# A fused attention and gated MLP block: the second x tile is issued from GpSimd's DMA queue instead of SyncE's

## The chip, the core and the metric

The kernel runs on one core of a Trainium2 chip. A core has five engines with a queue of instructions each: TensorE (PE; its weight loads are listed as PEld), VectorE (DVE), ScalarE (ACT), GpSimd (POOL) and SyncE (SP), which only issues DMAs. SyncE, ScalarE and GpSimd can all issue DMAs; sixteen DMA engines carry them out. In the profile q1 is the queue of SyncE's DMAs, q10 that of ScalarE's and q0 that of GpSimd's. The metric is the device time of one execution in microseconds, as the median of several runs; lower is better. The profile is of one execution.

## What is computed

x has 2048 rows of 640 (bfloat16). The block adds to x a sliding dilated attention and a gated MLP, both on the normalised x:

```python
xn = _layernorm(x)                 # mean and variance over the 640 columns, no weights
qkv = xn @ wqkv                    # 640 x 1920; 32 heads of 20
idx = pos[:, None] - arange(8) * 2 # each row attends to itself and 7 earlier ones, 2 apart
attn = softmax(q . k[idx] * 20 ** -0.5)
A = (attn . v[idx]) @ wo           # 640 x 640
B = ((xn @ w_gate) * (xn @ w_up)) @ w_down   # 640 x 1536, 640 x 1536, 1536 x 640
return x + A + B
```

## The kernel before

Rows are worked on in 16 tiles of 128 (TS), columns of x in 5 chunks of 128 (NCH). The time falls into stages on TensorE, in this order: a start with dummy matmuls and the first tiles; the projections to Q, K and V; gate and up of the MLP, during which VectorE does the attention; the down projections with the output projection of the attention; the stores. No loop is left on the chip. Every operation is recorded in program order by `op` (line 97), which derives its waits from the tiles that it reads and writes; `emit` (line 158) then writes each engine's own list in that order. So an engine's instructions run in the order in which the program records them for that engine, and every DMA has a semaphore of its own that its readers wait on.

The start of the program, to which the change belongs:

- VectorE clears ZERO, EPSC, IDENT, KH's and VO's padding, MASK and MSK0 (lines 297 to 306). GpSimd turns IDENT into an identity matrix and MSK0 into a mask with one affine_select each (lines 300 and 307). Before these it has only four small constant memsets, and after them nothing until it issues the accumulating DMAs of the attention (`acc`, line 532).
- XST holds the x tiles in 13 slots. x tile 0 is loaded in two halves, one from SyncE and one from ScalarE (lines 325 to 327). Then SyncE issues, one after the other: x tile 1 (line 328, by `x_load` of line 310), the five chunks of the Q weights (`wqkv_load(0, c)`), x tiles 2 and 3, the five chunks of the K weights, x tiles 4 to 7, the V weights in one DMA, and x tiles 8 to 12. None of these waits for anything. Each goes through the helper `dma` (line 293), so that the profile lists all of them under L294. Each x tile and each weight chunk has 160 KB. Behind them on SyncE stand the DMA transposes of tile 4 and later (L423).
- TensorE begins with nine dummy matmuls on ZERO (`warm(9)`, L453). The layer norm of tile 0 runs on VectorE (statistics L372 and L378, L384, reciprocal L404, scaling L419), with the square root on ScalarE (L385). TensorE then transposes the five chunks of tile 0 with the help of IDENT (`ln_pe`, L434), and VectorE copies them into XNT (L445).
- The statistics of tile 1 are ScalarE's work: `ln_sums` takes the sum (L392), the sum of squares (L394) and the square root (L397) from XST's slot 1; VectorE follows with the reciprocal and the scaling in two parts (L419, 256 and 384 columns).
- `proj_tile(0, 0, ...)` (L492) multiplies tile 0 with the Q weights: chunk after chunk, five matmuls each, 25 in all. Just before the five of the last chunk the program places `tr(1)`, the transposes of tile 1 and their copies. Then `proj_tile(0, 1, ...)` does the same for tile 1, and the loop at L773 multiplies tiles 0 and 1 with the K weights, with the transposes of tiles 2 and 3 in between.

Of the kernel before, what the change touches and what calls it, by code (L numbers as in the profile page):

```python
# [21 lines left out]
TS = 128  # L22
# [19 lines left out]
class Sched:  # L42
# [54 lines left out]
    def op(self, eng, fn, r=(), w=(), dma=False, name="", group=None, event=None):  # L97
        X = _Op()
        X.eng, X.fn, X.name, X.dma = eng, fn, name, dma
        X.needs_tick, X.event, X.pre_know, X.idx = False, None, None, len(self.ops)  # L100
        rk = [k for a in r for k in self.keys(a)]
        wk = [k for a in w for k in self.keys(a)]
        deps = {}
        inorder = eng in ("pe", "act", "dve")
        for k in rk:
            st = self.state.get(k)
            if st is not None:
                for o in st[0]:
                    deps[o.idx] = o
        for k in wk:  # L110
            st = self.state.get(k)
            if st is None:
                continue
            if group is not None and st[2] == group and not st[1]:
                for o in st[3]:
                    deps[o.idx] = o
                continue
            for o in st[0]:
                if not (eng == "pe" and o.eng == "pe"):
                    deps[o.idx] = o  # L120
            for q in st[1]:
                if eng in ("pe", "act") and q.eng == eng and not q.dma:
                    continue
                deps[q.idx] = q
        last = {}
        keep = []
        for d in deps.values():
            if d.dma or d.eng == "pool":
                keep.append(d)
            else:  # L130
                b = last.get(d.eng)
                if b is None or b.idx < d.idx:
                    last[d.eng] = d
        X.deps = keep + list(last.values())
        for d in X.deps:
            if not d.dma:
                d.needs_tick = True
        for k in rk:
            st = self.state.get(k)
            if st is None:  # L140
                self.state[k] = [[], [X], None, []]
            elif inorder and st[1] and st[1][-1].eng == eng and not st[1][-1].dma:
                st[1][-1] = X
            else:
                st[1].append(X)
        for k in wk:
            st = self.state.get(k)
            if group is not None and st is not None and st[2] == group and not st[1]:
                st[0].append(X)
            else:  # L150
                before = [] if st is None else st[0] + st[1]
                self.state[k] = [[X], [], group, before]
        if dma:
            X.event = event or self.dma_event(1)
        self.ops.append(X)
        return X
# [55 lines left out]
def build_kernel(nc, A_x, A_wqkv, A_wo, B_x, B_w_gate, B_w_up, B_w_down, out):  # L212
    K = Sched(nc)
    op = K.op
# [3 lines left out]
    def sb(name, shape, dtype=BF16, at=None):  # L218
        n = mybir.dt.size(dtype)
        for s in shape[1:]:  # L220
            n *= s
        n = (n + 63) // 64 * 64
        if at is None:
            at = place[0]
            place[0] += n
        assert at + n <= 229344, (name, at + n)
        return K.sbuf(name, shape, dtype, at)
# [37 lines left out]
    XST = sb("XST", [128, NXS, D], at=a_log)  # L265
# [24 lines left out]
    xhbm = A_x[0]  # L290
    ohbm = out[0]

    def dma(o, i, r=(), w=(), name="", eng="sp", group=None):
        return op(eng, lambda e: e.dma_start(o, i), r=r, w=w, dma=True, name=name, group=group)  # L294


    op("dve", lambda e: e.memset(ZERO[:], 0.0), w=[ZERO[:]], name="zero")  # L297
    op("dve", lambda e: e.memset(EPSC[:], EPS), w=[EPSC[:]], name="epsc")  # L298
    op("dve", lambda e: e.memset(IDENT[:], 0.0), w=[IDENT[:]], name="ident0")
# [10 lines left out]
    def x_load(t, eng="sp"):  # L310
        dma(XST[:, t % NXS, :], xhbm[t * TS:(t + 1) * TS, :], w=[XST[:, t % NXS, :]], name=f"xld{t}", eng=eng)
# [13 lines left out]
    for half, eng in ((0, "sp"), (1, "act")):  # L325
        dst = XST[:, 0, half * DHALF:(half + 1) * DHALF]
        dma(dst, xhbm[0:TS, half * DHALF:(half + 1) * DHALF], w=[dst], name=f"xh{half}", eng=eng)
    x_load(1)
    for c in range(NCH):
        wqkv_load(0, c)  # L330
    x_load(2)
# [622 lines left out]
def bass_parallel_sum__sliding_local_dilated__glu_gated_bilinear__prompt_kernel(  # L954
    nc, A_x, A_wqkv, A_wo, B_x, B_w_gate, B_w_up, B_w_down, out
):
    build_kernel(nc, A_x, A_wqkv, A_wo, B_x, B_w_gate, B_w_up, B_w_down, out)
# [28 lines left out]
```

## Time and profile before

| what | value |
|---|---|
| median of 4 runs | 252.63 us (252.48 to 252.7) |
| the profiled execution | 252.6 us |
| its span, first to last instruction | 251.3 us |
| mean granted TensorE clock | 1.000 |
| TensorE's idle time listed by its own waits | 1.0 us, at the start |
| weight loads' idle time listed before 8 us | 1.0 + 2.0 (dummy matmuls), 0.9, 0.2 us |
| GpSimd busy before 40 us | four memsets and two affine_selects (0.29 and 0.33 us) |
| DMA from SyncE's queue in the first 30 us | 10400 packets, 6.47 MB |

The table's busy shares and waits are of one execution. The page cuts the span in 40 slices of 6.28 us; the first one, to which the change belongs, and the two after it look like this (start of each row of the page, busy share in tenths):

| row | slices 1 to 3 |
|---|---|
| PE | 8 9 9 |
| DVE | 5 8 9 |
| ACT | 5 4 8 |
| POOL | 1 0 0 |
| DMA | 6 9 9 |

A line of the timeline gives the start and the duration in us, the engine, the line of the program, the operation, what it writes and reads, and how many instructions are merged; in brackets stand the idle time of that engine before it and what ended it. Issues of DMAs are marked by SPq, ACTq or POOLq; their duration is that of the issue and not of the transfer. The time from issue to landing comes from the DMA view.

### The profile page before, as it was taken

How to read it: one execution, taken by the hardware profiler on the slowest of the kernel's cores; microseconds unless marked ns; L12 is line 12 of the kernel's file. 1: busy time of each engine (PE TensorE's matmuls, PEld its weight loads, DVE VectorE, ACT ScalarE, POOL GpSimd, SP SyncE). 2: the span in 40 equal slices, each digit the busy share in tenths (PEclk: the TensorE clock that was granted, in tenths of full speed). 3: DMA queues.
4: the chain of work that ended last, by engine and by line, in shares of the span. 5: the costliest groups of instructions: out<-in, count | busy, mean ns of one | idle time of the engine just before them, and what ended most of it. 6: DMA issues, size and time to landing. Idle time of an engine off the chain costs nothing.

```text
span 251.3 us, 3265 instructions
## 1 busy us (share of the span) xinstructions
PE 248.4 (99%) x1294; PEld 129.2 (51%) x1294; DVE 215.9 (86%) x255; ACT 114.6 (46%) x203; POOL 32.6 (13%) x41
## 2 busy tenths in 40 slices
PE   8999999999999999999999999999999999999997
PEld 3995555555544444444444444444444444445775
DVE  5899889999999963999999994899999999996212
ACT  5487657555555557555555552325555111011000
POOL 1000001044434231002231101002000000200200
PEclk9999999999999999999999999999999999999999
DMA  6999879764787462355369972197500011490551
GB/s 179 318 279 198 102 194 408 180 115 87 134 147 129 83 122 45 125 211 102 66 125 261 383 231 42 37 332 62 93 0 3 21 29 34 57 134 21 81 153 52
DMA packets 33776, 33.78 MB, mean 134 GB/s; under 512 B 17985, under 2 KB 30273, under 8 KB 33729
## 3 DMA queue, kind: packets, MB, share of 16 engines
q1 hardware_dynamic: 27280, 24.13, 34.3%
q0 software_dynamic: 6192, 9.31, 22.9%
q8 instruction: 10, 0.16, 0.3%
q10 hardware_dynamic: 288, 0.13, 0.2%
q14 instruction: 6, 0.04, 0.0%
HBM read 14.42 MB, written 4.59 MB: 76 GB/s over the span
## 4 chain that ended last, share of the span: by engine, by line
PE 99%; DVE 0%; issue 0%
PE PS L638 41%; PE PS L665 22%; PE PS L475 21%; PE PS L697 7%; PE PS L499 2%; PE PS L453 2%; PE PS L492 1%; PE PS L773 1%; PE PS L434 1%; DVE FOUT L701 0%; DVE ZERO L297 0%; DVE EPSC L298 0%
## 5 line engine op out<-in xcount | busy, mean ns | idle before, releaser
L638 PE MATMUL PS<-XNT,WG 128*128 128x512 bf16 x240 | 59.6, 379 | 0.0
L638 PE MATMUL PS<-XNT,WU 128*128 128x512 bf16 x240 | 59.6, 379 | 0.0
L475 PE MATMUL PS<-XNT,WQKV 128*128 128x512 bf16 x250 | 54.1, 379 | 0.0
L605 DVE TENSOR_TENSOR PVB<-VO,ATB 128x10240 f16<-128x10240 bf16 x8 | 43.9, 5489 | 0.2
L475 PEld LDWEIGHTS PS<-XNT,WQKV 128*128 128x128 bf16 x250 | 29.4, 118 | 24.4
L640 ACT ACTIVATE USX<-PS 128x512 bf16<-128x512 f32 x48 | 28.7, 597 | 22.6 <-PE PS L638 22.6
L638 PEld LDWEIGHTS PS<-XNT,WU 128*128 128x128 bf16 x240 | 23.5, 98 | 28.3
L638 PEld LDWEIGHTS PS<-XNT,WG 128*128 128x128 bf16 x240 | 23.5, 98 | 28.3
L600 DVE TENSOR_TENSOR PVB<-PVB 128x5120 f16<-128x5120 f16 (+1 forms) x16 | 34.5, 2156 | 0.3
L533 POOL DMA_DIRECT2D LOG<-PE x24 | 21.9, 925 | 58.4 <-DMA LOG<-PE 58.4
L640 ACT ACTIVATE HT<-PS 128x512 bf16<-128x512 f32 x36 | 21.5, 597 | 16.4 <-PE PS L638 16.4
L671 ACT ACTIVATE DT<-PS 128x512 f16<-128x512 f32 x15 | 8.9, 596 | 42.5 <-PE PS L665 42.5
L665 PE MATMUL PS<-HT,WD 128*128 128x512 bf16 x120 | 27.5, 379 | 0.0
L522 DVE TENSOR_TENSOR TMP<-QH,KH 128x2048 f16<-128x2048 bf16 x16 | 19.2, 1219 | 1.0 <-ACT KH L482 0.9
L665 PEld LDWEIGHTS PS<-HT,WD 128*128 128x128 bf16 x120 | 11.7, 98 | 14.2
L522 DVE TENSOR_TENSOR PP<-QH,KH 128x2048 f16<-128x2048 bf16 x16 | 18.9, 1219 | 0.0
L665 PE MATMUL PS<-VO,WO 128*128 128x512 bf16 x75 | 18.6, 379 | 0.0
L527 DVE TENSOR_TENSOR PP<-PP,TMP 128x4096 f16<-128x4096 f16 x8 | 18.3, 2291 | 0.2
L701 DVE TENSOR_TENSOR FOUT<-PS,XR 128x320 bf16<-128x320 f32 (+2 forms) x9 | 4.1, 455 | 15.3 <-PE PS L697 15.3
L533 POOL DMA_DIRECT2D PE<-PP x8 | 8.3, 1043 | 63.3 <-DVE PP L528 63.3
L482 ACT ACTIVATE VO<-PS 128x512 bf16<-128x512 f32 x20 | 11.9, 597 | 8.5 <-PE PS L475 8.5
L643 DVE TENSOR_TENSOR HT<-HT,USX 128x512 bf16<-128x512 bf16 x36 | 14.3, 417 | 1.7 <-ACT USX L640 1.7
(71 smaller groups left out, 222.1 us busy)
## 6 DMA issues: line engine op xcount, KB each, us to landing
PE<-PP POOLq DMA_DIRECT2D x8, 512.0 KB, 4.8
ATB<-LOG SPq DMA_DIRECT2D x8, 512.0 KB, 4.9
LOG<-PE POOLq DMA_DIRECT2D x24, 128.0 KB, 2.7
WG<-in_B_w_gate_dram SPq DMA_DIRECT2D x1, 1920.0 KB, 8.1
WU<-in_B_w_up_dram SPq DMA_DIRECT2D x1, 1920.0 KB, 14.7
WD<-in_B_w_down_dram SPq DMA_DIRECT2D x1, 1920.0 KB, 11.4
out_dram<-in_A_x_dram SPq DMA_DIRECT2D x1, 1920.0 KB, 10.6
out_dram<-FACC POOLq DMA_DIRECT2D x3, 640.0 KB, 6.9
```

Of the source, the lines that this page charges most:

```text
L475: op("pe", (lambda l, x, c: lambda e: e.matmul(PS[:, b, :], l, x, start=(c == 0), stop=(c == NCH - 1)))(l, x, c), r=[l, x], w=[PS[:, b, :] ...
L482: op("act", lambda e: e.activation(o, PS[:, b, :], ACT.Copy, scale=sc), r=[PS[:, b, :]], w=[o], name=f"pev{which}_{m}_{j}")
L522: return (1.22, lambda: op("dve", lambda e: e.tensor_tensor(o, qw, kw, ALU.mult), r=[q, k], w=[o], name=f"prod{h}_{p}_{c}"))
L527: (2.3, lambda: op("dve", lambda e: e.tensor_tensor(a, a, b, ALU.add), r=[a, b], w=[a], name=f"psum{h}_{p}")),
L533: op("pool", lambda e: e.dma_start(o, i, accum_op=ALU.add), r=[o, i], w=[o], dma=True, name=name)
L600: return lambda: op("dve", lambda e: e.tensor_tensor(o, x, y, ALU.add), r=[x, y], w=[o], name=f"{name}_{b}")
L605: lambda: op("dve", lambda e: e.tensor_tensor(PVB[:], vw, aw, ALU.mult), r=[v, a], w=[PVB[:]], name=f"pv_{b}")),
L638: op("pe", (lambda l, x, c: lambda e: e.matmul(PS[:, b, :], l, x, start=(c == 0), stop=(c == NCH - 1)))(l, x, c), r=[l, x], w=[PS[:, b, :] ...
L640: op("act", lambda e: e.activation(o, PS[:, b, :], ACT.Copy), r=[PS[:, b, :]], w=[o], name=f"guev{which}_{m}_{j}")
L643: h_pending.append(lambda: op("dve", lambda e: e.tensor_tensor(h, h, o, ALU.mult), r=[h, o], w=[h], name=f"h{m}_{j}"))
L665: op("pe", (lambda l, x, i: lambda e: e.matmul(PS[:, b, :], l, x, start=(i == 0), stop=(i == n - 1)))(l, x, i), r=[l, x], w=[PS[:, b, :]], ...
L697: op("pe", (lambda l, x, i, b, wid: lambda e: e.matmul(PS[:, b, 0:wid], l, x, start=(i == 0), stop=(i == n - 1)))(l, x, i, b, wid), r=[l, ...
```

## The change

The load of x tile 1 is taken out of SyncE's list and recorded ahead of everything else as a DMA of GpSimd. It moves the same 128 rows of x to the same slot of XST under the same name, and its readers wait for its semaphore as before. SyncE goes from its half of tile 0 straight to the weights; GpSimd's two affine_selects stand behind the new DMA. Nothing else is changed.

```diff
+    op("pool", lambda e: e.dma_start(XST[:, 1, :], xhbm[TS:2 * TS, :]), w=[XST[:, 1, :]], dma=True, name="xld1")
     op("dve", lambda e: e.memset(ZERO[:], 0.0), w=[ZERO[:]], name="zero")
     op("dve", lambda e: e.memset(EPSC[:], EPS), w=[EPSC[:]], name="epsc")
     op("dve", lambda e: e.memset(IDENT[:], 0.0), w=[IDENT[:]], name="ident0")
...
     for half, eng in ((0, "sp"), (1, "act")):
         dst = XST[:, 0, half * DHALF:(half + 1) * DHALF]
         dma(dst, xhbm[0:TS, half * DHALF:(half + 1) * DHALF], w=[dst], name=f"xh{half}", eng=eng)
-    x_load(1)
     for c in range(NCH):
         wqkv_load(0, c)
```

## The prediction

> **What bounds the kernel now.** I read the page first. TensorE is busy 99% of the span, and the chain that ended last is TensorE from end to end.
>
> ```profile
> PE 248.4 (99%) x1294; PEld 129.2 (51%) x1294; DVE 215.9 (86%) x255; ACT 114.6 (46%) x203; POOL 32.6 (13%) x41
> PE 99%; DVE 0%; issue 0%
> ```
>
> So only something that moves TensorE's own stream can move the end. Next I read the waits of TensorE and of its weight loads: all of them lie in the first 8 us. From 8 us on the matmuls follow each other without a gap (the chain gives 250 of L475 in 53.96 us, 0.216 us each, and the same pace for L638 and L665). What the first 8 us gain or lose is therefore what the end gains or loses, unless later slack swallows it. Third, the timeline of those 8 us (start, duration, engine, idle before and its releaser):
>
> ```profile
> 0.74 0.86 SPq L294 DMA_DIRECT2D XST<-in_A_x_dram  x2
> ...
> 1.65 2.33 SPq L294 DMA_DIRECT2D WQKV<-in_A_wqkv_dram  x5
> ...
> 2.72 0.49 DVE L372 BATCH_NORM_STATS2 STATS<-XST 128x6 f32<-128x320 bf16 x1 [1.42 <-DMA XST<-in_A_x_dram]
> ...
> 3.92 0.29 ACT L385 ACTIVATE SD<-MV,EPSC 128x1 f32<-128x1 f32 x1 [1.68 <-DVE MV L384]
> ...
> 4.12 0.72 ACT L392 ACTIVATE XNS<-XST 128x640 bf16<-128x640 bf16 x1
> ...
> 5.64 1.18 PEld L492 LDWEIGHTS PS<-XNT,WQKV 128*128 128x128 bf16 x15
> ...
> 6.44 0.63 DVE L419 TENSOR_SCALAR XNS<-XST,MV,SD 128x256 bf16<-128x256 bf16 x2
> ...
> 7.03 0.32 PEld L492 LDWEIGHTS PS<-XNT,WQKV 128*128 128x128 bf16 x5 [0.21 <-DVE XNS L419]
> 7.29 0.32 PEld L434 LDWEIGHTS PS<-IDENT,XNS 128*128 128x128 bf16 x5
> ```
>
> SyncE issues half of x tile 0 (0.74), x tile 1 (about 1.2), then the five chunks of the Q weights, 0.47 us apart from 1.65. ScalarE takes the sums of x tile 1 from 4.12; VectorE normalises that tile at 6.44 to 7.07; TensorE transposes it at 7.29. The 0.21 us of idle before 7.03 is put down to VectorE, but those five matmuls (tile 0, chunk 3) don't read what L419 wrote. They read weight chunk 3. Fourth, the DMA view with one issue in each window (operands, queue, count, KB, us from issue to landing): x tile 1, then weight chunks 0, 3 and 4.
>
> ```profile
> XST<-in_A_x_dram SPq DMA_DIRECT2D x1, 160.0 KB, 2.7
> ...
> WQKV<-in_A_wqkv_dram SPq DMA_DIRECT2D x1, 160.0 KB, 2.9
> ...
> WQKV<-in_A_wqkv_dram SPq DMA_DIRECT2D x1, 160.0 KB, 3.9
> ...
> WQKV<-in_A_wqkv_dram SPq DMA_DIRECT2D x1, 160.0 KB, 3.9
> ```
>
> Chunk 3 is issued at about 3.07 and lands at 6.97: that releases 7.03. Chunk 4 (3.54) lands at 7.44, used at 7.57. Tile 1 lands at about 3.9, 0.2 before ScalarE wants it.
>
> **What the Trainium skill says.** "DMA: Bandwidth & Descriptors", Specifications, gives a first byte after about 1 us for a DMA issued by GpSimd and 0.6 us for one of SyncE. The trace has both later: SyncE's issue at 0.74 has its first packets at 1.76; GpSimd's at 51.04, on idle DMA engines, at about 2.45 minus 1.04, that is 1.4 us after its issue. The same page, Queues, rings and completion order, says that a DMA engine goes round the queues packet by packet. The trace agrees only in part: once running, GpSimd's queue shares the engines (56% to 57% from 136.3 to 139.2), but with a deep SyncE backlog it first waits:
>
> ```profile
> DMA packets 986, 1.21 MB, mean 242 GB/s; under 512 B 16, under 2 KB 986, under 8 KB 986
> ...
> q1 hardware_dynamic: 986, 1.21, 88.1%
> ...
> WD<-in_B_w_down_dram SPq DMA_DIRECT2D x1, 1920.0 KB, 11.4
> LOG<-PE POOLq DMA_DIRECT2D x2, 128.0 KB, 7.2
> ```
>
> This is the DMA view from 131.2 to 136.2. A GpSimd DMA was issued at 131.20; in 5 us not one packet of its queue ran. It landed after 7.2 us, where the same 128 KB land after 2.7 us on idle engines:
>
> ```profile
> LOG<-PE POOLq DMA_DIRECT2D x1, 128.0 KB, 2.7
> ```
>
> "SBUF — State Buffer", SBUF: two separate sides, says that VectorE in its two-port modes keeps GpSimd from writing descriptors. VectorE runs only memsets up to 1.3 us and then waits until 2.72; no run here shows such a lock, and I cost it at nothing.
>
> **The change part by part.**
> Removed from SyncE: one issue of 0.47 us. Everything that SyncE issues behind it before its first real wait (five Q chunks, x tiles 2 and 3, five K chunks, the later x tiles, the V weights) is issued 0.47 us earlier; the transposes at 14.04 wait for VectorE and stay with it. Issue isn't landing: the DMA engines are 0.8 to 1.0 busy from 2 us on, and the landings of the five Q chunks (4.55, 5.2, 6.2, 6.97, 7.44) lie up to 1.0 us apart where the issues are 0.47. The bytes in front of chunk 3 are the same before and after. I take 0.1 to 0.3 us of earlier landing for chunks 3 and 4, with 0 and 0.47 as the ends.
>
> What this is worth: if chunk 3 is there at 6.75, its matmuls follow at once (their pitch is 0.055 us), and the transposes of tile 1 could start at 7.03 instead of 7.29: 0.26 us. The next limits are close: the second part of L419 ends at 7.07, wanted by the third transpose at about 7.15, and chunk 4 (7.44, wanted at 7.31). So the gain is 0 to 0.26; I take 0.15. Further on, tile 2 lands at 7.82 and VectorE starts on it at 7.88; tile 2's normalisation ends at 10.31 for a transpose at 10.53; so 0.15 us passes through even if tile 2 lands no earlier. Where it is earlier, VectorE follows. Nothing later takes the gain: the gapless stream starts there.
>
> Added to GpSimd: one DMA issue. GpSimd is free at about 0.7. Issues of 128 KB are 0.86 to 0.88 us; the first one in the trace, of another shape, took 1.02 where its later ones start at 0.84, so I allow 1.05. Behind it in order stand two affine_selects: IDENT's goes from 1.27 to about 1.8, done near 2.1, and its first reader is the transpose at 4.81, 2.7 us of cover; MSK's output is read after 32 us.
>
> Moved: tile 1's data. First packet at 0.7 + 1.4 + 0.2 = 2.3, against about 2.4 before. In front then stand only the two halves of tile 0 (ScalarE's first packets at 2.08, both landed by 3.1) and weight chunk 0, posted at about 1.2 + 1.0 = 2.2. From below: tile 1 goes first and lands as it does now, 3.9. From above within this mechanism: it waits for chunk 0 and then shares with chunk 1. 160 KB at half of about 250 GB/s take 1.3 us, from 3.2, plus 0.3 until the last of 16 engines reports: 4.8. Alternating with chunk 0 from 2.4, by the same rate: 2.4 + 1.3 + 0.3 = 4.0 to 4.4. I take 4.2.
>
> What waits for it: ScalarE's L392 stands first in its queue, so sums, square, square root, then VectorE's reciprocal and L419, then everything of VectorE behind that, go with it. ScalarE is ready at 4.12. Each us past 4.12 moves L419 by as much; against today's 7.40 for the third transpose, L419's 7.13 leaves 0.27 us. So a landing up to 4.39 costs nothing against before, and after that the loss is landing minus 4.39. At 4.2 the loss is nothing; but L419 (7.13 + 0.08) allows a gain of 0.19.
>
> Sum for the profiled execution: 252.6 (span 251.3, and 1.3 around it) minus 0.15 is 252.45. The median of the runs is 252.63, 0.03 above it: 252.5.
>
> **The rivals.**
> A, the forecast: tile 1 lands by 4.4 and the weight wait shrinks, 252.35 to 252.65. For it: little is posted ahead at 2.3.
> B: both queues alternate to tile 1's cost, landing 4.4 to 4.9, lost 0 to 0.5: 252.6 to 253.1. For it: the even sharing seen at 136 us; five chunks follow without a pause. Against it: the shared stretch need only last 160 KB.
> C, the other side: GpSimd's queue is kept out by the SyncE stream. It decides from a landing of 4.9 on (4.39 + 0.5). Place: ScalarE's L392, price 1 us for each us. At 5.5 the end is 252.63 + 1.1 = 253.7; with the whole 7.2 us of issue to landing, 7.9 - 4.39 = 3.5, so 256.1. For it: three GpSimd issues under load (131.20, 132.57, 139.98) landed after 7 to 10 us. Against it: in those, 1.9 MB stood ahead; here some 0.3 MB at most.
> D: it does more than I see, for instance that TensorE's clock comes up earlier against the work. The pitch of the 128-wide matmuls is 0.107 us up to 6.2 and 0.055 after; the skill's "TensorE: Matmul & The Clock Gate", Part 1, calls the moment variable from run to run. The eleven or so matmuls at the slow pitch between 5.1 and 6.25, each 0.05 us dearer, bound this at 0.6 us: 252.0.
> That tile 1 isn't loaded in time for the sum to be right isn't a rival: ScalarE waits for its semaphore.
>
> **How the numbers follow.** A 0.42, B 0.20, C 0.30, D 0.08. About 0.2% (0.5 us) is what a measurement of this kernel can tell from no change. A and B stay within it except for their edges; C is slower; D is faster where it is whole. Faster 0.07, same 0.62, slower 0.31. The range goes from 252.3 (A's best) to 253.5, which takes in B and the near half of C and leaves out about 2 in 10 (most of D, the far end of C). The likeliest case alone has 252.35 to 252.65.
>
> **What would show it.** Tile 1's landing, and the idle before L392: none beyond the wait for the deviation of tile 0 if A holds, 1 us for each us in C. The five weight loads at 7.03 without their 0.21 us. IDENT's affine_select near 1.8 with no one waiting. SyncE's first weight issue at about 1.17. The start of L773 (9.38) earlier by 0.1 to 0.2 in A and later in B and C. The forecast is wrong if tile 1 lands after 4.9, or if chunks 3 and 4 land no earlier and tile 1 later.

## The result, and the profile after

The changed kernel takes 253.12 us (median of 32 runs, 252.57 to 253.72) where the kernel before, in runs beside it, takes 252.54 us (52 runs). The ratio is 1.0022 with a 95% interval of 1.0017 to 1.0027: about 0.6 us slower. The forecast was 252.5 us, a little faster or no change. The measured time lies within the range of 252.3 to 253.5, but on the other side of the kernel before, and clear of it.

The profiled execution took 253.23 us, with a span of 251.9. First the page of the changed kernel, the share of the last chain by engine:

```profile
PE 96%; DMA 2%; ACT 1%; DVE 1%; issue 0%
```

TensorE had 99% of this chain before. Now a DMA is in it. Its chain of waits in order of time (start, length, what) says which:

```profile
1.30 3.84 DMA XST<-in_A_x_dram
5.17 0.84 ACT XNS L392 x2
...
6.03 0.93 ACT XNS L394 x2
...
7.31 0.17 DVE SD L404
...
7.51 0.36 DVE XNS L419
...
7.91 0.28 PE PS L434 x2
```

Until 7.91 the end hangs on the load of tile 1, ScalarE's sums and VectorE's scaling; from there on it is TensorE as before. The timeline of the same kernel answers to the lines shown of the kernel before:

```profile
1.20 2.66 SPq L294 DMA_DIRECT2D WQKV<-in_A_wqkv_dram  x5
...
1.30 0.73 POOL L297 DMA_DIRECT2D XST<-in_A_x_dram  x1 [0.86 <-DVE MSK L307]
...
5.17 0.74 ACT L392 ACTIVATE XNS<-XST 128x640 bf16<-128x640 bf16 x1 [0.87 <-DMA XST<-in_A_x_dram]
...
6.91 0.32 PEld L492 LDWEIGHTS PS<-XNT,WQKV 128*128 128x128 bf16 x5 [0.18 <-issue]
...
7.51 0.64 DVE L419 TENSOR_SCALAR XNS<-XST,MV,SD 128x256 bf16<-128x256 bf16 x2
7.90 0.11 PEld L434 LDWEIGHTS PS<-IDENT,XNS 128*128 128x128 bf16 x2 [0.67 <-DVE XNS L419]
...
10.00 1.16 PEld L773 LDWEIGHTS PS<-XNT,WQKV 128*128 128x128 bf16 x11
```

SyncE's first weight issue starts at 1.20 instead of 1.65, and the weight loads of the chunk 3 matmuls at 6.91 instead of 7.03: this part of the change works. But ScalarE idles for 0.87 us until tile 1 is there and starts its sums at 5.17 instead of 4.12. The transposes of tile 1 follow at 7.90 instead of 7.29. The first K matmul, which closes the disturbed part, has its weight load at 10.00. In the kernel before the same line is

```profile
9.38 1.16 PEld L773 LDWEIGHTS PS<-XNT,WQKV 128*128 128x128 bf16 x11
```

The difference, 0.62 us, is the whole difference of the two profiled executions (253.23 against 252.6), but for 0.01 us. The rest is rigid: from this weight load to the end of the span it is 241.93 us in both.

The DMA view of the changed kernel, at GpSimd's issue, gives the tile's landing (1.30 + 3.8 = 5.1):

```profile
XST<-in_A_x_dram POOLq DMA_DIRECT2D x1, 160.0 KB, 3.8
```

The tile's packets run from 2.94 on. In the DMA view from 2.93 to 4.8, SyncE's queue (q1) has the larger share of the DMA engines beside them (queue, packets, MB, share):

```profile
q1 hardware_dynamic: 312, 0.35, 52.1%
q0 software_dynamic: 48, 0.16, 37.0%
```

### The profile page after: what moved, and what is told of

It reads as the page before. It is cut to its first block, busy times and chain, and to the rows that moved or that the text cites. A ratio compares the mean times of both kernels' runs of the same rounds, so it can differ in the third digit from the quotient of the medians.

```text
span 251.9 us, 3265 instructions
## 1 busy us (share of the span) xinstructions
PE 248.5 (99%) x1294; PEld 129.1 (51%) x1294; DVE 216.0 (86%) x255; ACT 114.6 (45%) x203; POOL 33.0 (13%) x42
## 4 chain that ended last, share of the span: by engine, by line
PE 96%; DMA 2%; ACT 1%; DVE 1%; issue 0%
PE PS L638 41%; PE PS L665 22%; PE PS L475 21%; PE PS L697 7%; PE PS L499 2%; DMA XST<-in_A_x_dram 2%; PE PS L773 1%; PE PS L492 1%; PE PS L434 0%; ACT XNS L394 0%; ACT XNS L392 0%; DVE XNS L419 0%; ACT SD L397 0%; DVE FOUT L701 0%; DVE SD L404 0%
```

## The experiments

In seven more kernels tile 1, or another transfer of the start, goes by another way, and two kernels are profiled a second time. The times are ratios to the kernel before in runs beside them; where there is only one execution, its profile is used.

**1. Tile 1 from ScalarE's queue.** GpSimd has no part in it; SyncE goes straight to the weights as in the changed kernel. The edit is made on the kernel before:

```diff
-    x_load(1)
+    x_load(1, eng="act")
     for c in range(NCH):
         wqkv_load(0, c)
```

> x tile 1 is issued by ScalarE right behind its half of tile 0, GpSimd issues nothing at the start, SyncE goes straight to the weights as in the changed kernel. Theory 1 (GpSimd's queue is what makes the tile late: late start, then a slow share of the engines): issue near 1.4 us, landing 3.9 to 4.4, ScalarE's sums start by 4.4, weight chunk 3 still earlier by about 0.1; time 0.0 to 0.2 us under the kernel before. Rival 2 (the tile is late because the weights are posted ahead of it and take the engines, whichever queue issues it): landing 4.8 to 5.1 as in the changed kernel, time 0.4 to 0.6 us over the kernel before.

Measured: 253.09 us against 252.64, ratio 1.0016 (1.0008 to 1.0024). So most of the loss is there without GpSimd. But the profiled execution took only 252.56, the second fastest of these 22 runs. In its timeline the sums wait for 0.40 us:

```profile
4.49 0.74 ACT L392 ACTIVATE XNS<-XST 128x640 bf16<-128x640 bf16 x1 [0.40 <-DMA XST<-in_A_x_dram]
```

Neither theory has its numbers: the profile lies near the first (a wait until 4.49, where it allowed 4.4), the times fit the rival. Hence a second profile of the same kernel.

> A second look at the kernel with tile 1 on ScalarE's queue, whose profiled execution (252.56) was faster than most of its timed ones (median 253.09). If its landing varies from one execution to the next, tile 1 lands at another time than 4.47 here and the first K matmul follows it; if the spread comes from elsewhere (the moment at which TensorE's clock comes up), the landing is near 4.5 again and the span minus the start of L773 isn't 241.93.

It took 253.35 us, and the same line is now

```profile
5.28 0.74 ACT L392 ACTIVATE XNS<-XST 128x640 bf16<-128x640 bf16 x1 [1.02 <-DMA XST<-in_A_x_dram]
...
10.11 0.94 PEld L773 LDWEIGHTS PS<-XNT,WQKV 128*128 128x128 bf16 x9
```

The first K weight load is at 10.11 instead of 9.33; the span minus that start is 241.93 in both. The tile landed 0.8 us apart in the two executions (4.47 and 5.26), and the time follows it. They ran on two chips, so part of that may belong to the chip. One profile of such a kernel does not stand for its median.

**2. VectorE's memsets out of GpSimd's way.** GpSimd's DMA began at 1.30, just when VectorE's last memset ended, and the profile names that memset as what released it. On the changed kernel the last four of VectorE's seven memsets are made to wait for GpSimd's identity matrix (one of them shown):

```diff
-    op("dve", lambda e: e.memset(MASK[:], 0.0), w=[MASK[:]], name="mask0")
+    op("dve", lambda e: e.memset(MASK[:], 0.0), r=[IDENT[:]], w=[MASK[:]], name="mask0")
```

> The changed kernel with VectorE's last four memsets (padding and masks) made to wait for GpSimd's identity matrix, so that VectorE is idle from about 1.03 us until then. Theory 3 (VectorE's memsets hold the port that GpSimd needs to write descriptors): GpSimd's DMA starts near 1.0 instead of 1.30, the tile lands near 4.8 instead of 5.14, time about 0.3 us under the changed kernel. Rival (0.6 us is what a first GpSimd DMA takes to be dispatched): start at 1.30 as before, landing 5.0 to 5.3, time as the changed kernel.

```profile
1.30 0.73 POOL L297 DMA_DIRECT2D XST<-in_A_x_dram  x1 [0.85 <-DVE IDENT L300]
```

The start stays at 1.30 though VectorE is idle from 1.03. The program gives this DMA nothing to wait for, and the bracket now names another memset with the start unmoved: the name in it was no cause. The ratio is 1.0021 (1.0013 to 1.0030), as in the changed kernel. So these four memsets don't hold the DMA up; the first three, which end by 1.03, run here too and are not tested. The last chain of this kernel shows the time before the start (POOLq is GpSimd's sequencer, which hands out its instructions):

```profile
0.62 0.02 POOLq L971
0.64 0.65 issue
...
1.30 4.00 DMA XST<-in_A_x_dram
```

GpSimd's sequencer is past the opening of the program at 0.64. "issue" is time without a wait that the profile shows.

**3. The weights wait for tile 1.**

```diff
-        wqkv_load(0, c)
+        wqkv_load(0, c, r=[XST[:, 1, :]] if c == 0 else ())
```

(`wqkv_load` hands `r` on to `dma`; the change is made on the changed kernel.)

> The changed kernel, but SyncE's first weight chunk, and so everything behind it, waits until tile 1 has landed: tile 1 meets only the two halves of tile 0 on the DMA engines. If sharing with the weights makes it late: start 1.30, first packets near 2.9, landing 3.6 to 4.0. If GpSimd's own path is slow whatever else runs: landing 4.7 or later. The time itself is worse by 1 to 2 us, since the weights are issued only then.

```profile
XST<-in_A_x_dram POOLq DMA_DIRECT2D x1, 160.0 KB, 2.6
```

Same start, 1.30, and a landing at 3.9 instead of 5.1. In this one profile the company of the weights is worth 1.2 us. Without that company the tile lands as early as in the kernel before (3.9), late start and all, and the sums start at 4.24 without waiting for it. So the late start by itself costs nothing here. The one time, 254.59 us, is 2.0 us over the profile of the kernel before, the top of what was expected: the weights are issued only from 3.93 on.

**4. One place further back on SyncE.** On the kernel before, no GpSimd DMA:

```diff
+    wqkv_load(0, 0)
     x_load(1)
-    for c in range(NCH):
+    for c in range(1, NCH):
         wqkv_load(0, c)
```

> The kernel before with SyncE's order of tile 1 and weight chunk 0 swapped: no GpSimd DMA. Theory of the price (a landing up to about 4.4 is free, each us after that costs a us): tile 1 is issued at about 1.65 and lands at 4.5 to 4.8, so the time is 0.1 to 0.4 us over the kernel before. Rival (only a GpSimd DMA costs anything, through GpSimd or the ring): no change, within 0.1 us.

```profile
4.50 0.74 ACT L393 ACTIVATE XNS<-XST 128x640 bf16<-128x640 bf16 x1
...
9.34 1.16 PEld L774 LDWEIGHTS PS<-XNT,WQKV 128*128 128x128 bf16 x11
```

A landing at about 4.5 costs nothing that can be told: ratio 1.0004 (0.9995 to 1.0012), which takes in no change and does not exclude 0.3 us. The expected 0.1 to 0.4 us is thus neither confirmed nor excluded at its low end. (Its lines are numbered one higher from L393 on.)

**5. Two places further back on SyncE.** Again on the kernel before:

```diff
-    x_load(1)
     for c in range(NCH):
+        if c == 2:
+            x_load(1)
         wqkv_load(0, c)
```

> The kernel before with tile 1 two places further back on SyncE, behind weight chunks 0 and 1, and no GpSimd DMA: the same lateness by another queue. If the landing alone sets the price (free up to about 4.4, then a us for a us, less what the earlier weights give), tile 1 is issued at 2.1, lands at 5.0 to 5.5 and the time is 0.5 to 0.9 us over the kernel before, as much as in the changed kernel. If something of GpSimd's queue adds to the loss there, this one stays at 0.3 or under with the same landing.

```profile
5.49 0.74 ACT L393 ACTIVATE XNS<-XST 128x640 bf16<-128x640 bf16 x1 [1.11 <-DMA XST<-in_A_x_dram]
...
10.32 0.72 PEld L774 LDWEIGHTS PS<-XNT,WQKV 128*128 128x128 bf16 x7
```

The ratio is 1.0042 (1.0028 to 1.0055), about 1.1 us (0.7 to 1.4), where 0.5 to 0.9 was expected. A late landing costs time by SyncE's queue too: nothing of GpSimd is needed for the loss.

**6. GpSimd's DMA with another load.** On the kernel before, GpSimd loads tile 2; tile 1 stays ahead of the weights on SyncE:

```diff
+    op("pool", lambda e: e.dma_start(XST[:, 2, :], xhbm[2 * TS:3 * TS, :]), w=[XST[:, 2, :]], dma=True, name="xld2")
...
     x_load(1)
     for c in range(NCH):
         wqkv_load(0, c)
-    x_load(2)
     x_load(3)
```

> The kernel before with tile 2 in tile 1's part: GpSimd's first instruction loads tile 2, which nobody needs before 7.8 us, and SyncE keeps tile 1 ahead of the weights. If the loss of the changed kernel is tile 1's landing alone, tile 1 lands at 3.9 to 4.2 again and most of the loss is gone; but 160 KB now share with the weights that used to be behind them, so chunks 3 and 4 land up to 0.5 us later than before (7.0 and 7.4) and the time is 0.1 to 0.5 us over the kernel before. Rival (a GpSimd DMA in the first us costs by itself, whatever it moves): 0.6 us over, with tile 1 and the weights landing as before.

```profile
XST<-in_A_x_dram SPq DMA_DIRECT2D x1, 160.0 KB, 2.3
XST<-in_A_x_dram POOLq DMA_DIRECT2D x1, 160.0 KB, 3.6
```

Tile 1 lands at 1.2 + 2.3 = 3.5, tile 2 by GpSimd at 1.3 + 3.6 = 4.9. The sums of tile 1 don't wait for it, and K begins as in the kernel before:

```profile
4.05 0.72 ACT L392 ACTIVATE XNS<-XST 128x640 bf16<-128x640 bf16 x1
...
9.41 1.16 PEld L773 LDWEIGHTS PS<-XNT,WQKV 128*128 128x128 bf16 x11
```

The ratio is 1.0006 (0.9997 to 1.0014). So the DMA on GpSimd by itself costs nothing that these runs can tell, and under 0.4 us; the rival with its 0.6 us is out. The first theory holds for tile 1, but not its reason for a small loss: chunks 3 and 4 landed at 7.0 and 7.4, not later than before, with 160 KB more sharing the engines ahead of them.

**7. A weight chunk from ScalarE's queue.** On the kernel before, tile 1 keeps its place; chunk 3, on which TensorE waits there, is issued by ScalarE at 2.26, after its first small activation, which writes DUM (`wqkv_load` hands `r` on as in experiment 3):

```diff
     for c in range(NCH):
-        wqkv_load(0, c)
+        if c == 3:
+            wqkv_load(0, c, eng="act", r=[DUM[:]])
+        else:
+            wqkv_load(0, c)
```

> The kernel before, with weight chunk 3 issued by ScalarE right after its first small activation (about 2.3 us) instead of by SyncE at 3.07; tile 1 keeps its place ahead of the weights on SyncE, GpSimd issues nothing. If a queue of its own lets a chunk overtake those in front of it: chunk 3 lands by 6.5, its matmuls follow without the 0.21 us of idle, tile 1 (in front of it by a us) still lands by 4.1, and the time is 0.1 to 0.3 us under the kernel before. Rival (the DMA engines are full, so that what one transfer gains the others lose): chunks 1, 2 or 4 come late in its place, the time is within 0.1 us or up to 0.3 over.

Its timeline has the wait of chunk 3 gone and two others in its place, at chunk 2 (6.44) and chunk 4 (7.52):

```profile
5.54 0.68 PEld L495 LDWEIGHTS PS<-XNT,WQKV 128*128 128x128 bf16 x10
6.44 0.60 PEld L495 LDWEIGHTS PS<-XNT,WQKV 128*128 128x128 bf16 x10 [0.22 <-DMA WQKV<-in_A_wqkv_dram]
...
7.52 0.55 PEld L495 LDWEIGHTS PS<-XNT,WQKV 128*128 128x128 bf16 x9 [0.22 <-DMA WQKV<-in_A_wqkv_dram]
```

Chunk 3 landed at 2.26 + 3.3 = 5.6, ahead of chunk 2 (about 6.4). The ratio is 0.9999 (0.9991 to 1.0007): no gain. The rival had it right: chunk 3 came earlier, and TensorE waited for chunks 2 and 4 in its place. No version here beats the kernel before.

**8. The changed kernel profiled again.**

> A second look at the changed kernel. GpSimd's DMA starts at 1.30 again if its start is fixed; tile 1's landing shows how far it varies (5.14 in the first look). The end stays 241.93 us after the first K matmul in either case.

GpSimd's DMA starts at 1.31, the sums at 5.07, the first K weight load at 9.91; 253.14 us. The first profile was no exception.

**The profiles together.** S is the start of ScalarE's sums of tile 1, K the first weight load of the K projection, both from the timelines. Experiments 3 and 7, which move the weights themselves, are left out:

| kernel | tile 1 by | S | K | K - S |
|---|---|---|---|---|
| tile 2 by GpSimd | SyncE | 4.05 | 9.41 | 5.36 |
| before | SyncE | 4.12 | 9.38 | 5.26 |
| tile 1 by ScalarE, first profile | ScalarE | 4.49 | 9.33 | 4.84 |
| one place back | SyncE | 4.50 | 9.34 | 4.84 |
| changed, second profile | GpSimd | 5.07 | 9.91 | 4.84 |
| changed, first profile | GpSimd | 5.17 | 10.00 | 4.83 |
| tile 1 by ScalarE, second profile | ScalarE | 5.28 | 10.11 | 4.83 |
| memsets late | GpSimd | 5.32 | 10.16 | 4.84 |
| two places back | SyncE | 5.49 | 10.32 | 4.83 |

From 4.49 on K is S plus 4.83 or 4.84, whichever queue brings the tile. In the first two rows something else sets K near 9.4; in the kernel before that is weight chunk 3, for which TensorE waits just ahead of the transposes of tile 1. The two meet at S = 9.38 - 4.84 = 4.54. That is the price of a late tile 1: nothing until 4.5, then a us for a us.

## Why the prediction was wrong, point by point

- **Where the time is decided: right.** The first 10 us decide; it is 241.92 to 241.94 us from K to the end in every profile of the table.
- **SyncE's part: right in kind; the size was luck.** The weight loads of chunk 3 start 0.12 us earlier in the first profile, inside the 0.1 to 0.3 forecast. But there the issue of chunk 2 took 0.78 us instead of 0.43, so that the five issues end at 3.86 (1.20 + 2.66) instead of 3.98: little of the 0.47 us that the forecast took as removed was left for chunk 3 and what follows. In the second profile they end at 3.51, and chunk 3's weight loads start at 6.51, half a us earlier and outside the forecast. Nothing of it is left in the end, since the transposes of tile 1, which stand next on TensorE, wait for L419.
- **GpSimd's start, the first term that failed.** The prediction had "GpSimd is free at about 0.7" and took that for the start of its DMA. The sequencer is free then (0.64), but the DMA starts at 1.30. The 1.6 us from there to the first packet came true, so the packet put at 2.3 came at 2.94: 0.64 us late. By the forecast's own sum this alone moves the landing from 4.2 to 4.8. In the profile of the kernel before no operation of GpSimd starts between 0.34 and 1.27, so nothing there bore out the 0.7. Experiment 2 takes VectorE's last four memsets out of question; what fills the 0.6 us is not shown.
- **The share of the engines, the second term.** From the first packet to the landing the forecast put 1.9 us (2.3 to 4.2); it was 2.2 (2.94 to 5.14), 0.3 us more. The two terms make up the 0.94 us by which the landing missed. Against a price that begins at 4.5, this second term alone would have cost nothing and the first alone 0.3 us; it took both for 0.6. Experiment 3 shows what the weights' company is worth as a whole, 1.2 us, where the forecast reckoned with chunk 0 alone in the way. ScalarE's queue doesn't escape it either (landings of 4.47 and 5.26 in experiment 1). That the tile lost its place in front of the weights in one and the same queue fits this and experiments 4 and 5, but no run separates it from the mere number of bytes under way at the same time.
- **The price: right but for 0.1 us.** The prediction let a landing of 4.39 pass free and then charged a us for a us. The table has 4.5 and the same slope. For a landing of 5.14 this gives 0.6 us, which is the result.
- **The rivals.** The mechanism was B's: both queues shared the engines, at tile 1's cost. B's landing (4.4 to 4.9) was too early by 0.2 us, since it took over the early start; its times (252.6 to 253.1) all but reach the result. By the landing alone the result lies in C's part, from 4.9 on, but C's cause is not what the trace shows: GpSimd's queue was not kept out for microseconds as behind the 1.9 MB at 131 us. It started late and then shared. D explains none of the loss: K follows S by 4.83 or 4.84 us in all seven profiles with a late tile. That 253.12 us lies within the stated range is due to B and C, not to the forecast's own case.
- **IDENT's delay: right that it is harmless.** The affine_select went from 1.27 to 2.12 (1.8 forecast), and TensorE's first transpose at 4.90 doesn't wait for it; it waits for VectorE, which is 0.09 us later since ScalarE's half of tile 0 landed that much later.

What stays open: why GpSimd's DMA starts at 1.30, and what an earlier start would have saved beside the weights; no run has one. The changed kernel and the one with ScalarE's queue, which is issued at about 1.4, have overlapping intervals (1.0017 to 1.0027 and 1.0008 to 1.0024), and the landing of the latter was 4.47 once and 5.26 once.

## What to carry to other kernels

A queue is also an order: one and two places further back in SyncE's queue tile 1 landed at 4.5 and 5.5 instead of 3.9. A transfer that is taken out of the line in front of others, to start them sooner, no longer stands in front of them; if it is the one that is wanted first, it pays for the sharing even where it is issued only 0.1 to 0.2 us later, as here. So ask of a moved load when it is wanted, how much slack it has (here 0.6 us, from a landing at 3.9 to 4.5), and what will be on the DMA engines with it. Leave the load without slack in its place; one with slack can move (tile 2 cost nothing that could be told), though here it gained nothing either.

## What the runs showed that I had not expected

- The first DMA of GpSimd starts at 1.30 to 1.31 in all five profiles that have one there, with its sequencer free from 0.64.
- GpSimd's DMA of 160 KB is cut otherwise than SyncE's. The page of the changed kernel has 48 packets more on q0 and 144 fewer on q1 than before (6192 and 27280):

```profile
q1 hardware_dynamic: 27136, 23.97, 34.4%
q0 software_dynamic: 6240, 9.47, 23.0%
```

- A tile on ScalarE's queue beside the weights landed 0.8 us apart in two profiles (4.47 and 5.26), while behind chunk 0 in SyncE's queue it costs nothing that can be told from no change.
